# The first stage of an attention and two-layer feed-forward kernel, done by pairs of batches

## The chip, the cores and the metric

The kernel runs on one core of a Trainium2 chip. The metric is the device time of one execution in microseconds (us); several runs give a median. Five engines work side by side, each through its own instruction list in order: TensorE (PE in the rows; PEld is its weight load), VectorE (DVE), ScalarE (ACT), GpSimd (POOL) and SyncE (SP), which issues most transfers.

## The reference

Attention over 4 batches, 8 heads, 576 tokens and 64 channels, through 32 memory slots, feeds a gated feed-forward layer (1536 wide) and then a second layer (2048 wide). All in float32; the feed-forward weights arrive as 64-bit numbers.

```python
a = exp(phi - max(phi, axis=2)); a = a / (sum(a, axis=2) + 1e-09)
k_m = einsum('bhsm,bhsd->bhmd', a, k);  v_m = einsum('bhsm,bhsd->bhmd', a, v)
attn = softmax(q @ k_m.T / 8);          x = attn @ v_m          # to (2304, 512)
xn = x / sqrt(mean(x * x) + 1e-06) * rms_g
x = (silu(xn @ w_gate) * (xn @ w_val)) @ w_out
h = x @ w_in
g = where(h >= 1, h, where(h <= -1, 0, (h + 1) ** 2 / 4))
out = g @ w_out2
```

## The kernel before

**Precision.** A product of float32 matrices is made of three matmuls with operands split in a high and a low part: high by high, high by low, low by high. A 64-bit weight block of 512 KB (`raw`, four buffers) is turned into float32 by `convert` in four elementwise steps: high word scaled (line 271 or 273), low word scaled (276 or 278), merged (282), sign put in (287, always VectorE before, since `BIAS["VAsign"]` is 98.9). Where the weight is also split, ScalarE makes the high and VectorE the low part (301, 303).

**Attention.** For each batch b, `soft` takes the softmax numerators of phi, `memory` the products k_m and v_m, and `pair` handles 128 rows by two tokens of queries: scores, softmax, squares for the norm, and at last the normalized attention weights `Ah`, `Al` (transposes `ATp`, lines 717 to 728). There are eight full pairs and one for the last 64 tokens of all four batches (`RESTS`, `ORDER`).

**Gates.** The attention output is never formed. Instead v_m is multiplied into the gate and value weights: `vw` makes, from two weight chunks of 128 columns and one batch, the products `vwps` (line 772), which are split into `vwh` and `vwl`. `gv` multiplies these by `Ah`, `Al`: per batch and chunk two halves of 288 tokens, a `gps` and a `vps` group of 6 matmuls each (line 819). So there are 4 x 12 x 2 x 2 = 192 such groups, 1152 matmuls of 288 columns. `gate` applies the silu and at once splits the result into `ah`, `al` (lines 872 to 893), for which there are 12 buffers. The converted chunks are written to DRAM (`wf_d`) and read back for batches 1 to 3, 36 times 512 KB.

**out1.** Per batch, block of 128 output columns and half, a group of 36 matmuls of 288 columns (line 920), 1152 in all. `x2_parts` splits the result and writes it to DRAM. Meanwhile the second layer's weights are converted and written to `w_d` (`w2_piece`).

**Second stage.** `p2_in` (`hp`, line 1098) and `p2_out` (`acc`, line 1129) run over four blocks of 512 tokens and one of 256. Its weights come back through POOL's queue; twelve of them wait until the first stage's matrices have left their place (`w2b`).

**Order.** All of the first stage is written by one planner, `Agenda`: generator streams ask for an engine and a time, for buffers (`take`, `give`) or for flags, and the planner emits instructions in the order in which they could start by its own costs, ties by priority (`P_GV` 850, `P_OUT1` 900). The chip then runs each engine's list in that order. Before, weight loading begins after the exponentials of batch 3 (`W_AFTER`), and out1 after the attention.

Of the kernel before, what the change touches and what calls it, by code (L numbers as in the profile page):

```python
# [7 lines left out]
F32 = mybir.dt.float32  # L8
# [6 lines left out]
P = 128  # L15
# [8 lines left out]
BUFS = {"phi": 2, "kv": 2, "q": 2, "qr": 1, "pm": 1, "gm": 2, "s1": 2, "kd": 2, "qT": 2, "e": 4, "aT": 3, "half": 1, "raw": 4, "x": 2, "w": 3, "vw": 2, "a": 12, "th": 2, "xs": 3, "w2s": 2}  # L24
RESTS = [[0, 1, 2, 3]]
ORDER = [0, 1, 2, 3, 8, 4, 5, 6, 7]

BANKS = {"g": (0, 1), "v": (2, 3), "o": (4, 5), "p": (0, 1, 2, 3), "w": (6, 7), "q": (2, 3), "s": (1,), "x": (2, 3), "a": (0,), "t": (5,), "k": (7,), "m": (4,), "l": (4,)}

HEAT = (6, ('e', 2), 2.09, 0.34)  # L30
# [3 lines left out]
SHARE = {"VAhi", "VAsign", "Vs", "VGlo", "VGal", "GVe"}  # L34
# [8 lines left out]
Q_AT = [2, 6, 8, 9, 12]  # L43


class Agenda:
# [11 lines left out]
    def __init__(self, room):  # L58
        self.room = dict(room)
        self.turn = {}  # L60
        self.ticks = {}
        self.flags = {}
        self.free = {"D": 1.7}
        self.now = 0.0
        self.port = 0.0
        self.done = 0.0
        self.live = []
        self.count = 0
# [23 lines left out]
    def _start(self, x):  # L92
        kind, arg = x[3]
        at = x[4]
        if kind == "take":
            return (at, None) if self.room[arg] else None
        if kind == "flag":
# [18 lines left out]
    def run(self, stop=None):  # L116
        while self.live and not (stop and stop in self.flags):
# [14 lines left out]
            if kind == "take":  # L132
                self.room[arg] -= 1
            elif kind == "give":
                self.room[arg] += 1
            elif kind == "rest":
# [28 lines left out]
def tile_attn_moe(tc, q, k, v, phi, w_gate, w_val, w_out1, rms_g, w_in2, w_out2, out):  # L165
# [45 lines left out]
    def bank(tag, name):  # L211

        n = turn[tag] = turn.get(tag, -1) + 1
        z = BANKS[tag][n % len(BANKS[tag])]
        yield "take", ("bank", z)
        return psum.tile([P, 512], F32, tag=f"b{z}", name=name), ("bank", z)

    turn = {}
# [13 lines left out]
    keep = pool(right, "keep", "right")  # L232
# [5 lines left out]
    Ah = [keep.tile([P, 2, S], F32R, tag=f"Ah{b}", name=f"Ah{b}", bufs=1) for b in range(B)]  # L238
    Al = [keep.tile([P, 2, S], F32R, tag=f"Al{b}", name=f"Al{b}", bufs=1) for b in range(B)]

    agenda = Agenda({**BUFS, **{("bank", z): 1 for z in range(8)}})
# [9 lines left out]
    def convert(src, pieces, dst, split, done):  # L251
# [7 lines left out]
        nc.sync.dma_start(out=rs.rearrange("p (c f) -> p c f", c=pieces) if pieces > 1 else rs, in_=src)  # L259
        yield "rest", DMA_LAG  # L260
# [35 lines left out]
        if split:  # L296
            hi, lo = split
# [16 lines left out]

    apart = list(range(BUFS["w"], BUFS["w"] + BUFS["w2s"]))

# [31 lines left out]
    inputs = ExitStack()  # L348
    ld = pool(inputs, "ld", "left")
    st = pool(att, "st", "right")  # L350
    phi_t, kv_t, q_t = {}, {}, {}
    kmT_t = [st.tile([P, H, 2, M], F32, name=f"kmT{b}") for b in range(B)]
# [15 lines left out]
    def loads():  # L368

        seq = []  # L370
        for b in range(B):
            seq += [("phi", b), ("kv", b)]
        for i, pr in zip(Q_AT, q_loads, strict=True):
            seq.insert(i, ("q", pr))
        for s in seq:
            yield "take", "qr" if s[0] == "q" and s[1][0] == B else s[0]
# [5 lines left out]
            elif s[0] == "kv":  # L382
                b = s[1]
                t = kv_t[b] = ld.tile([P, 2, 4, J, D], F32, tag="kv", name=f"kv{b}", bufs=BUFS["kv"])
# [5 lines left out]
            else:  # L390
                b = s[1][0]
                yield "Dq", 3.4 if b < B else 0.45 * len(per_batch(s[1]))
                if b == B:
                    t = q_t[s[1]] = ld.tile([P, H, LJ, D], F32, tag="qr", name=f"qr{s[1][1]}", bufs=BUFS["qr"])
                    for bb, rows in per_batch(s[1]):
# [814 lines left out]
```

## Time and profile before

| | |
|---|---|
| median of 3 runs | 844.69 us (842.64 to 846.34) |
| span of the profiled execution, first to last instruction | 842.8 us |
| busy: PE, PEld, DVE, ACT, POOL | 97%, 85%, 53%, 40%, 10% |
| mean granted TensorE clock | 0.989 |
| moved by transfers | 137.54 MB |

The profiled execution has no run time of its own in the records, only its span; the median of the runs is 1.9 us above it. Two neighbouring matmuls overlap in the records, so the pace of a series is read from its length and count, and not from the duration of one.

### The profile page before, as it was taken

To read this page: it belongs to the slowest core of one execution; us is meant where nothing else is said; L and a number is where in the kernel's file an instruction comes from. 1 tells how busy PE (TensorE), PEld (TensorE's weight loads), DVE (VectorE), ACT (ScalarE), POOL (GpSimd) and SP (SyncE) were. 2 spreads that over 40 slices of the span, in tenths; PEclk is the share of its full clock that TensorE was granted. 3 is DMA by queue.
4 is the path that set the end of the run, shared out by engine and by line. 5 is a ranking of instruction groups with operands and counts; after the bars stand their busy time and mean duration, and the time that the engine had idled before them with its cause. 6 is when DMAs were issued, how large, how long until landed. Compare 5 with 4: busy or idle time off the path is not lost.

```text
span 842.8 us, 14911 instructions
## 1 busy us (share of the span) xinstructions
PE 819.2 (97%) x6052; PEld 719.6 (85%) x6052; DVE 450.7 (53%) x788; ACT 336.7 (40%) x635; POOL 82.6 (10%) x133
## 2 busy tenths in 40 slices
PE   7999879999999999999999999999999999999997
PEld 5887767999999998999998888888888888888896
DVE  3678898985775577558214333433343334333443
ACT  1558866763663356436203222222222222222232
POOL 3365400100000000001305100000000000000000
PEclk9999899999999999999999999999999999999999
DMA  9974697885789767886979900100040003000100
GB/s 319 323 248 134 217 313 259 301 281 182 241 281 305 237 217 261 265 265 224 327 233 343 368 1 1 51 1 0 10 141 0 1 1 101 0 1 1 51 1 25
DMA packets 76804, 137.54 MB, mean 163 GB/s; under 512 B 9408, under 2 KB 46272, under 8 KB 76736
## 3 DMA queue, kind: packets, MB, share of 16 engines
q1 hardware_dynamic: 66080, 108.02, 38.9%
q0 software_dynamic: 10496, 28.32, 10.6%
q8 instruction: 47, 0.77, 0.4%
q10 hardware_dynamic: 160, 0.26, 0.1%
q14 instruction: 21, 0.17, 0.1%
HBM read 99.35 MB, written 37.22 MB: 162 GB/s over the span
## 4 chain that ended last, share of the span: by engine, by line
PE 90%; DMA 5%; ACT 2%; DVE 2%; issue 1%; SPq 0%; ACTq 0%; DVEq 0%
PE acc L1129 24%; PE hp L1098 24%; PE ops L920 18%; PE vps L819 8%; PE gps L819 7%; PE vwps L772 2%; PE xp L693 2%; DMA raw<-in_moe_w_val_dram 2%; PE sc L630 2%; DMA raw<-in_moe_w_gate_dram 1%; DMA kv<-in_v_dram 1%; PE kvps L504 1%; DMA raw<-in_moe_w_out_dram 1%; PE qps L612 1%; PE heat L484 1%
## 5 line engine op out<-in xcount | busy, mean ns | idle before, releaser
L1098 PE MATMUL hp<-xh,w 128*128 128x512 f32 (+1 forms) x640 | 193.2, 368 | 0.0
L1129 PE MATMUL acc<-w,gh 128*128 128x512 f32 x576 | 178.4, 391 | 0.0
L1098 PEld LDWEIGHTS hp<-xh,w 128*128 128x128 f32 x640 | 117.0, 188 | 21.5
L1104 DVE SCALAR_TENSOR_TENSOR y<-y 128x512 f32<-128x512 f32 (+1 forms) x80 | 51.1, 638 | 151.4 <-ACT y L1103 151.4
L1129 PEld LDWEIGHTS acc<-w,gh 128*128 128x128 f32 x576 | 107.0, 188 | 22.5
L1098 PE MATMUL hp<-xl,w 128*128 128x512 f32 (+1 forms) x320 | 118.3, 370 | 0.0
L920 PE MATMUL ops<-ah,wo1h 128*128 128x288 f32 x384 | 113.7, 296 | 0.0
L920 PE MATMUL ops<-ah,wo1l 128*128 128x288 f32 x384 | 113.1, 295 | 0.0
L920 PE MATMUL ops<-al,wo1h 128*128 128x288 f32 x384 | 113.1, 294 | 0.0
L1129 PE MATMUL acc<-w,gl 128*128 128x512 f32 x288 | 112.6, 392 | 0.0
L1103 ACT ACTIVATE y<-hp,consts 128x512 f32<-128x512 f32 (+1 forms) x80 | 51.6, 645 | 151.2 <-PE hp L1098 151.2
L1113 ACT ACTIVATE gh<-y 128x512 fp32r<-128x512 f32 (+1 forms) x80 | 47.5, 593 | 137.4 <-PE acc L1129 120.0
L1114 DVE TENSOR_TENSOR gl<-y,gh 128x512 fp32r<-128x512 f32 (+1 forms) x80 | 51.1, 639 | 80.3 <-ACT gh L1113 80.3
L920 PEld LDWEIGHTS ops<-ah,wo1h 128*128 128x128 f32 x384 | 72.0, 188 | 2.5 <-issue 2.5
L920 PEld LDWEIGHTS ops<-al,wo1h 128*128 128x128 f32 x384 | 72.0, 188 | 0.0
L920 PEld LDWEIGHTS ops<-ah,wo1l 128*128 128x128 f32 x384 | 72.0, 188 | 0.0
L1098 PEld LDWEIGHTS hp<-xl,w 128*128 128x128 f32 x320 | 60.3, 188 | 10.7
L1129 PEld LDWEIGHTS acc<-w,gl 128*128 128x128 f32 x288 | 54.0, 188 | 12.3
L819 PE MATMUL vps<-Ah,vwh 128*128 128x288 f32 x192 | 59.6, 310 | 3.0 <-DVE th L875 2.9
L819 PE MATMUL gps<-Ah,vwh 128*128 128x288 f32 x192 | 58.3, 303 | 1.5 <-ACT th L872 1.5
L819 PE MATMUL gps<-Ah,vwl 128*128 128x288 f32 x192 | 57.3, 298 | 0.0
L819 PE MATMUL gps<-Al,vwh 128*128 128x288 f32 x192 | 57.2, 298 | 0.0
(123 smaller groups left out, 1258.1 us busy)
## 6 DMA issues: line engine op xcount, KB each, us to landing
w<-wf_d SPq DMA_DIRECT2D x36, 512.0 KB, 4.9
w<-w_d POOLq DMA_DIRECT2D x36, 512.0 KB, 10.5
w_d<-w2s SPq DMA_DIRECT2D x32, 512.0 KB, 3.9
raw<-in_moe_w_out_dram SPq DMA_DIRECT2D x28, 512.0 KB, 5.0
raw<-in_moe_w_in_dram SPq DMA_DIRECT2D x16, 512.0 KB, 5.5
raw<-in_moe_w_gate_dram SPq DMA_DIRECT2D x12, 512.0 KB, 5.2
raw<-in_moe_w_val_dram SPq DMA_DIRECT2D x12, 512.0 KB, 6.3
wf_d<-w SPq DMA_DIRECT2D x12, 512.0 KB, 4.0
```

Source lines behind the costliest of these rows:

```text
L484: nc.tensor.matmul(out=t[:, 0:256], lhsT=zeros[:, 0:P], rhs=zeros, start=True, stop=True, skip_group_check=True,)
L630: nc.tensor.matmul(out=scv[rows, z, :], lhsT=qT[:, h, rows], rhs=kmT_t[bb][:, z].rearrange("p j m -> p (j m)"), start=True, stop=True, ski ...
L693: nc.tensor.matmul(out=xp[rows, 256 * g : 256 * g + 256], lhsT=aT[:, i, g, rows], rhs=vbd_t[bb][:, g].rearrange("p h d -> p (h d)"), start ...
L772: nc.tensor.matmul(out=vps[g][0][32 * c : 32 * c + 32, 2 * P * x : 2 * P * x + 2 * P], lhsT=vT[b][hs, c, :], rhs=t[hs, c].rearrange("p i f ...
L819: nc.tensor.matmul(out=p[:, 0:HB], lhsT=wt[:, g, i, :], rhs=at[b][:, g, c], start=(g == 0 and x == 0), stop=(g == 1 and x == 2),)
L920: nc.tensor.matmul(out=p[:, 0:HB], lhsT=wt[:, fc, d], rhs=at[:, c], start=(fc == 0 and x == 0), stop=(fc == NF1 - 1 and x == 2),)
L1098: nc.tensor.matmul(out=hp, lhsT=wt[:, kc, :], rhs=xt[:, kc, 0:n], start=(kc == 0 and x == 0), stop=(kc == KC - 1 and x == 2),)
L1103: nc.scalar.activation(out=y, in_=hp, func=AF.Relu, scale=0.5, bias=half)
L1104: nc.vector.scalar_tensor_tensor(out=y, in0=y, scalar=1.0, in1=y, op0=ALU.min, op1=ALU.mult)
L1113: nc.scalar.activation(out=gh, in_=y, func=AF.Copy)
L1114: nc.vector.tensor_tensor(out=gl, in0=y, in1=gh.bitcast(F32), op=ALU.subtract)
L1129: nc.tensor.matmul(out=acc, lhsT=gt[:, cs], rhs=wt, start=(fc == 0 and x == 0), stop=(fc == NF2 - 1 and x == 2),)
```

## The change

Only the first stage is changed.

- `vw` takes one chunk and both batches of a pair (0 and 1, then 2 and 3); `gv` runs chunk by chunk over the two batches. A converted chunk is read back 12 times, not 36. Two `w` buffers remain of three.
- The last tokens are done by two pairs instead of one: for batches 0 and 1 after their own pairs, for 2 and 3 at the end.
- Loads follow `LOADS`: four weight blocks are asked for before phi, k and v of batch 2. Weight conversion may begin after the first batch's keys (`W_AFTER`).
- The sign step may go to ScalarE and POOL (`BIAS["VAsign"]` 0.5); it does so for 24 of 68 blocks.
- `soft` takes the maximum of phi by halving (`fold`, four operations) instead of one strided reduction.
- A gate stays unsplit, in the places of the inputs k, v and phi (`th_free`), and is split when out1 needs it (`splits`, three buffers `ab`). k and v of batch 2 have a place of their own, which becomes `Ah`, `Al` of batches 2 and 3 (`late`).
- out1 runs per batch over 512 tokens, all four output blocks at once in four banks, and at last over the 256 remaining tokens: 576 matmuls of 512 columns and 144 of 256. The results are written in 40 transfers instead of 96.
- Any free bank of a list is picked instead of the next in turn.

```diff
-RESTS = [[0, 1, 2, 3]]
-ORDER = [0, 1, 2, 3, 8, 4, 5, 6, 7]
...
+RESTS = [[0, 1], [2, 3]]
+ORDER = [0, 1, 2, 3, 8, 4, 5, 6, 7, 9]
...
-W_AFTER = [("e", 3)]
+W_AFTER = [("km", 0)]
...
-BIAS = {"VAhi": -0.0664, "GAlow": -0.8, "VGlo": 0.3, "VGsum": -99, "GVe": 0.8, "VGal": 0.3, "VAsign": 98.9, "VGvbd": -0.169}
+BIAS = {"VAhi": -0.0664, "GAlow": -0.8, "VGlo": 0.3, "VGsum": -99, "VGmax": 0, "GVe": 0.8, "VGal": 0.3, "VAsign": 0.5, "VGvbd": -0.169}
...
+LOADS = [
+    ("phi", 0), ("kv", 0), ("q", 0), ("phi", 1), ("kv", 1), ("q", 2), ("q", 4), ("raw", 3), ("phi", 2), ("kv", 2),
+    ("phi", 3), ("kv", 3), ("q", 5), ("q", 7), ("q", 9)
+]
...
+            if s[0] == "q":
+                add(-1, load_q(s))
+                continue
+            if s[0] == "raw":
+                yield "flag", s
+                continue
...
+                place = {"tag": "late", "bufs": 1} if b == 2 else {"tag": "kv", "bufs": BUFS["kv"]}
+                t = kv_t[b] = (late if b == 2 else ld).tile([P, 2, 4, J, D], F32, name=f"kv{b}", **place)
...
+        for z in range(BUFS["kv"]):
+            yield "take", "kv"
+            t = ld.tile([P, 9, SM], F32, tag="kv", name=f"kvth{z}", bufs=BUFS["kv"])
+            if z == 0:
+                rest.append(t.rearrange("p n s -> p (n s)")[:, 0 : NF1 * NL].rearrange("p (n s) -> p n s", n=NF1))
+            for y in range(6 if z == 0 else 0, 9):
...
+    def fold(name, x, to, op, kind):
+
+        eng = yield kind, (1.75, 3.2)
+        e = nc.vector if eng == "V" else nc.gpsimd
+        t = st.tile([P, 4, 4, M], F32, tag="half", name=f"half{name}", bufs=BUFS["half"])
+        e.tensor_tensor(out=t, in0=x[:, :, 0:4], in1=x[:, :, 4:8], op=op)
+        e.tensor_tensor(out=t[:, :, 0:2], in0=t[:, :, 0:2], in1=t[:, :, 2:4], op=op)
+        e.tensor_tensor(out=to, in0=t[:, :, 0], in1=t[:, :, 1], op=op)
+        e.tensor_tensor(out=to, in0=to, in1=x[:, :, 8], op=op)
+        yield "give", "half"
...
                     )
-        yield "give", "kv"
+        if b != 2:
+            yield "give", "kv"
+        else:
+            t = late.tile([P, 2, 2, 2, S], F32R, tag="late", name="late2", bufs=1)
+            for y, x in enumerate((Ah, Al)):
+                x.update({2: t[:, y, 0], 3: t[:, y, 1]})
+            mark("late")
...
     def vw():
 
-        for n in range(0, NT, 2):
-            b = n // NF1
-            yield "flag", ("vT", b)
+        for n in range(NP * NF1):
+            pb = n // NF1 * 2
             for x in range(2):
-                yield "flag", ("w", n + x)
...
+            yield "Pw", 1.05
+            t = w_t.pop(n)
             for x in range(2):
...
-
+        for n in range(NP * NF1):
+            fc = n % NF1
+            for x in range(2):
+                b = n // NF1 * 2 + x
+                if fc == 0:
+                    for jj in range(2):
+                        yield "flag", ("A", (b, jj))
...
+                for hf in range(2):
+                    if hf:
+                        yield "flag", ("A", (B, [b in r for r in RESTS].index(True)))
+                        yield "flag", ("th", 0)
...
+                    add(P_GV, gate(b, fc, hf, ps))
+                mark(("gv", b, fc))
+            yield "give", "vw"
...
+        for b in range(B + 1):
+            n = SM if b < B else NL
+            for fc in range(NF1):
+                for hf in range(2):
+                    yield "flag", ("g", min(b, B - 1), fc, hf)
+                yield "take", "ab"
+                t = p1x.tile([P, 2, SM], F32R, tag="ab", name=f"ab{b}_{fc}", bufs=BUFS["ab"])
+                ah, al = t[:, 0, 0:n], t[:, 1, 0:n]
+                src = th_t[b, fc] if b < B else rest[0][:, fc]
+                yield "A", 0.16 + n / 1150
+                nc.scalar.activation(out=ah, in_=src, func=AF.Copy)
+                add(P_GV, low_part(b, fc, src, ah, al))
...
     def out1():
-        for b in range(B):
-            for d4 in range(KC):
-                yield "flag", ("wo1", d4 // 2)
-                for hf in range(2):
-                    c = slice(HB * hf, HB * hf + HB)
-                    p, p_bank = yield from bank("p" if b == B - 1 and d4 else "o", f"ops{b}_{d4}_{hf}")
-                    for fc in range(NF1):
...
-                        d = slice(P * d4, P * d4 + P)
-                        for x, (wt, at) in enumerate(((wo1h, ah), (wo1h, al), (wo1l, ah))):
-                            nc.tensor.matmul(
-                                out=p[:, 0:HB], lhsT=wt[:, fc, d], rhs=at[:, c],
-                                start=(fc == 0 and x == 0), stop=(fc == NF1 - 1 and x == 2),
-                            )
-                        if d4 == KC - 1 and hf:
-                            add(P_OUT1, give("a"))
-                    add(P_OUT1, x2_parts(b, d4, hf, p[:, 0:HB], p_bank))
-
...
+            acc = []
+            for fc in range(NF1):
+                yield "flag", ("wo1", fc)
+                yield "flag", ("a", b, fc)
+                ah, al = a_t.pop((b, fc))
+                for d4 in range(KC):
+                    if fc == 0:
+                        acc.append((yield from bank("o", f"ops{b}_{d4}")))
+                    p, p_bank = acc[d4]
...
+                    if fc == NF1 - 1:
+                        add(P_OUT1, x2_parts(b, d4, n, p[:, 0:n], p_bank))
+                yield "give", "ab"
+
...
     add(P_VW, load_w())
-    for z in range(2):
-        for u in range(NF1 // 2):
```

The first place is SP's list, from the loads of the second batch's k and v on (`phi_381` before and `phi_604` of the change are phi of batch 2, `kv_402` and `kv_606` its k and v). Before:

```order
L381 DMA phi_381<-in_phi_dram 128x4x288
L402 DMA q_400<-in_q_dram 128x8x256
L387 DMA kv_402<-in_k_dram 128x4x576
L387 DMA kv_402<-in_v_dram 128x4x576
L396 DMA qr_585<-in_q_dram 32x8x128 x4
L402 DMA q_611<-in_q_dram 128x8x256
L381 DMA phi_711<-in_phi_dram 128x4x288
L387 DMA kv_713<-in_k_dram 128x4x576
L387 DMA kv_713<-in_v_dram 128x4x576
L402 DMA q_824<-in_q_dram 128x8x256
```

Of the change, where the first weight block, a query block and the last tokens' queries stand just ahead of these rows:

```order
L276 DMA raw_520<-in_moe_w_val_dram 128x4x256
L276 DMA raw_548<-in_moe_w_gate_dram 128x4x256
L276 DMA raw_574<-in_moe_w_val_dram 128x4x256
L276 DMA raw_589<-in_moe_w_gate_dram 128x4x256
L406 DMA phi_604<-in_phi_dram 128x4x288
L413 DMA kv_606<-in_k_dram 128x4x576
L413 DMA kv_606<-in_v_dram 128x4x576
L406 DMA phi_718<-in_phi_dram 128x4x288
L413 DMA kv_720<-in_k_dram 128x4x576
L413 DMA kv_720<-in_v_dram 128x4x576
L365 DMA wf_d<-w_388 128x1024
L447 DMA q_915<-in_q_dram 128x8x256
```

Four weight blocks, and a fifth that reuses the first one's buffer, now stand ahead of batch 2's phi, k and v, and the store of chunk 0 ahead of the last two query blocks.

The second place is TensorE's list in the gates, where the end of one group, one `vw` and the next work stand. Before (chunks `w_1564` and `w_1645`, batch 0's `vT_89`):

```order
L819 MATMUL vps_0_1756<-Al_97,vwh_1624 128x288
L819 MATMUL vps_0_1756<-Ah_93,vwl_1625 128x288
L772 MATMUL vwps_0_1763<-w_1564,vT_89 32x256 x4
L772 MATMUL vwps_1_1764<-w_1564,vT_89 32x256 x4
L772 MATMUL vwps_0_1763<-w_1645,vT_89 32x256 x4
L772 MATMUL vwps_1_1764<-w_1645,vT_89 32x256 x4
L819 MATMUL gps_1_1776<-Ah_93,vwh_1624 128x288
L819 MATMUL gps_1_1776<-Al_97,vwh_1624 128x288
L819 MATMUL gps_1_1776<-Ah_93,vwl_1625 128x288
```

Of the change (chunk `w_936`, `vT_92` and `vT_93` of batches 0 and 1):

```order
L875 MATMUL vps_2_1_1779<-Al_99,vwh_1553 128x288
L875 MATMUL vps_2_1_1779<-Ah_97,vwl_1554 128x288
L826 MATMUL vwps_0_1789<-w_936,vT_92 32x256 x4
L826 MATMUL vwps_1_1790<-w_936,vT_92 32x256 x4
L826 MATMUL vwps_0_1789<-w_936,vT_93 32x256 x4
L826 MATMUL vwps_1_1790<-w_936,vT_93 32x256 x4
L967 MATMUL ops_0_1819<-ab_0_1642,wo1h 128x512 x2
L967 MATMUL ops_0_1819<-ab_0_1642,wo1l 128x512
L875 MATMUL gps_3_0_1826<-Ah_96,vwh_1678 128x288
L875 MATMUL gps_3_0_1826<-Al_98,vwh_1678 128x288
```

The same four rows now use one chunk for two batches, and groups of out1 with 512 columns stand between the gates from the fourth chunk on.

## Rows read from the trace of the kernel before

**Rows 1.** The page's head and part 1: busy time, share, instructions.

```profile
span 842.8 us, 14911 instructions
PE 819.2 (97%) x6052; PEld 719.6 (85%) x6052; DVE 450.7 (53%) x788; ACT 336.7 (40%) x635; POOL 82.6 (10%) x133
```

**Rows 2.** Busy time by stretches: stretch, length, busy by engine, clock, DMA share, rate.

```profile
core 0: us, PE busy (x) PEld busy (x) DVE busy (x) ACT busy (x) POOL busy (x), PEclk, DMA share, GB/s
0.00:41.80 41.80, 35.28 (x520) 29.11 (x528) 20.47 (x42) 13.93 (x24) 14.53 (x35) 0.96 1.03 320
41.80:106.00 64.20, 59.03 (x778) 50.27 (x773) 50.38 (x99) 48.92 (x106) 34.79 (x45) 0.92 0.62 201
106.00:140.30 34.30, 28.27 (x269) 24.03 (x269) 30.90 (x58) 22.11 (x44) 0.00 (x0) 0.95 0.82 273
140.30:176.20 35.90, 35.90 (x388) 32.40 (x386) 32.25 (x58) 25.90 (x53) 3.05 (x4) 1.00 0.88 310
176.20:441.10 264.90, 264.25 (x2294) 254.73 (x2287) 157.98 (x284) 121.35 (x241) 13.68 (x22) 1.00 0.78 255
441.10:842.80 401.70, 396.45 (x1825) 329.02 (x1823) 158.71 (x250) 104.46 (x170) 16.55 (x28) 1.00 0.18 58
```

**Rows 3.** The chain that ended last, pieces: start, length, engine, tile, line, count.

```profile
213.40 0.80 PE gps L819 x6
215.00 0.79 PE gps L819 x6
243.31 1.02 PE vwps L772 x32
244.34 0.99 PE vps L819 x6
400.96 40.16 PE ops L920 x303
441.12 10.22 PE hp L1098 x45
460.21 2.72 PE acc L1129 x12
457.47 2.75 PE hp L1098 x12
800.89 1.44 PE hp L1098 x12
```

**Rows 4.** The chain between 92 and 140 us, its four longest pieces.

```profile
97.96 6.44 DMA raw<-in_moe_w_gate_dram
...
105.86 5.02 DMA raw<-in_moe_w_gate_dram
...
122.45 5.82 DMA raw<-in_moe_w_val_dram
...
129.07 6.92 DMA raw<-in_moe_w_val_dram
```

**Rows 5.** TensorE by line until 105.2 us, and the attention's last transposes.

```profile
L819 PE MATMUL gps<-Ah,vwh 128*128 128x288 f32 x10 | 3.9, 390 | 0.0
L819 PE MATMUL vps<-Ah,vwh 128*128 128x288 f32 x8 | 2.8, 349 | 0.0
L772 PE MATMUL vwps<-w,vT 64*32 64x256 f32 x64 | 2.2, 382 | 0.0
...
L717 PE MATMUL ATp<-ident,e x36: 272/273/329, 43.8 to 105.1; 128*128 128x128 f32 x36
```

**Rows 6.** TensorE and VectorE by line, 106 to 140.3 us.

```profile
L819 PE MATMUL vps<-Ah,vwh 128*128 128x288 f32 x27 | 9.1, 337 | 2.3 <-DVE th L875 2.2
L819 PE MATMUL gps<-Ah,vwh 128*128 128x288 f32 x26 | 8.4, 322 | 1.5 <-ACT th L872 1.5
L772 PE MATMUL vwps<-w,vT 64*32 64x256 f32 x112 | 4.2, 385 | 2.3 <-DVE w L287 2.3
L287 DVE SCALAR_TENSOR_TENSOR w<-raw,w 128x512 uint32<-128x512 uint32 x13 | 8.8, 682 | 0.0
```

**Rows 7.** VectorE, SP and POOL in order of time: start, length, line, operation.

```profile
34.22 0.68 DVE L646 TENSOR_TENSOR e<-sc,mx 128x512 f32<-128x512 f32 x1
41.78 0.69 DVE L640 TENSOR_REDUCE mx<-sc 128x16 f32<-128x512 f32 x1 [1.55 <-PE sc L630]
76.04 2.24 DVE L282 SCALAR_TENSOR_TENSOR w<-w,raw 128x512 uint32<-128x512 uint32 x2
76.23 1.50 POOL L664 TENSOR_TENSOR e<-e,sm 128x512 f32<-128x512 f32 x1
444.17 0.53 POOL L1031 DMA_DIRECT2D w<-w_d  x1 [26.86 <-PE hp L1098]
```

More of the change, by code (lines that the diff above doesn't have):

```diff
@@ L211, in bank @@
     def bank(tag, name):
-        n = turn[tag] = turn.get(tag, -1) + 1
-        z = BANKS[tag][n % len(BANKS[tag])]
-        yield "take", ("bank", z)
+        early = BANKS.get(tag + "0") if "attention" not in agenda.flags else None
+        z = yield "pick", early or BANKS[tag]
         return psum.tile([P, 512], F32, tag=f"b{z}", name=name), ("bank", z)
-    turn = {}
     base = pool(top, "base", "left")
@@ L296, in convert @@
         if split:
+            if place:
+                yield "take", place
+                split = split()
             hi, lo = split
@@ L406, in loads @@
-            add(0, arrived(s))
-        for name in ("phi", "kv", "q", "qr"):
-            for _ in range(BUFS[name]):
-                yield "take", name
-        mark("inputs")
+            add(0, arrived(s))
+        for z in range(BUFS["kv"]):
[4 more added lines that the diff above has]
+            for y in range(6 if z == 0 else 0, 9):
+                th_free.append(t[:, y])
+                yield "give", "th"
+            mark(("th", z))
@@ L582, in memory, with spread_v @@
         mark(("vT", b))
+    def spread_v(b, vs):
+        vbd = vbd_t[b]
+        for g in range(2):
+            eng = yield "VGvbd", (0.41, 0.62)
+            (nc.vector if eng == "V" else nc.gpsimd).tensor_tensor(
+                out=vbd[:, g],
+                in0=vs[:, g].unsqueeze(1).to_broadcast([P, 4, D]),
+                in1=mask.unsqueeze(2).to_broadcast([P, 4, D]),
+                op=ALU.mult,
+            )
+        mark(("vbd", b))
+        yield "give", "kd"
     def per_batch(pr):
@@ L966, in tile_attn_moe, with wo1_unit @@
-    wo1_left = [NF1 // 2, NF1 // 2]
+        rows, c = slice(P * d4, P * d4 + P), slice(SM * b, SM * b + n)
+        for x, dst in ((xh, x2h_d), (xl, x2l_d)):
+            yield "D", 0.7
+            nc.sync.dma_start(out=dst[rows, c], in_=x.bitcast(F32))
+        yield "rest", DMA_LAG
+        xs_free.append(tag)
+        yield "give", "xs"
+    def wo1_unit(fc):
+        if fc:
+            yield "flag", ("wo1 begun", fc - 1)
+        mark(("wo1 begun", fc))
+        src = wbits["out1"][P * fc : P * fc + P, :]
+        yield from convert(src, 1, None, (wo1h[:, fc], wo1l[:, fc]), lambda: mark(("wo1", fc)))
@@ L1005, in tile_attn_moe @@
         add(10**6, heat())
-    agenda.run("inputs")
-    inputs.close()
-    p1 = pool(left, "p1", "left")
-    th_free += [p1.tile([P, S], F32, name=f"th_{z}") for z in range(BUFS["th"])]
     add(P_GV, gv())
-    add(P_SOFT, more_places())
-    add(P_W2 - 1, more_w2s())
+    for b in range(2):
+        add(P_SOFT, more_xs(b))
     agenda.run("attention")
@@ L1076, in tile_attn_moe @@
     load_x(0)
-    for i in range(N2U, N2U + N2R):
-        load_w2(2 * i + 1, w2c)
     agenda.run()
```

360 lines of the change are left out of this document (161 added, 199 removed), and 5 rows, old and new, of the table BANKS.

## The prediction

> **What bounds the kernel now.** The page comes first: TensorE is busy 97% of the span [rows 1], but matmuls overlap in the records, so this doesn't show where it waits. The table of stretches splits the span where the work changes [rows 2]. From 441.1 us on runs the second stage, 401.7 us long, and the change doesn't touch it. From 140.3 us on TensorE is full in every stretch. What can be won lies in the attention, up to 106 us, in the stretch from 106 to 140.3 us, where it is busy 28.3 of 34.3 us, and in the pace of its full stretches.
>
> The pace is read from the chain [rows 3]. A gate group of 6 matmuls takes 0.797 us (0.80 and 0.79 in turn). A `vw` takes 1.02 us and makes the group behind it 0.19 us longer, so 1.21 us. In out1, 303 matmuls of 288 columns take 40.16 us, 132.5 ns each. In the second stage 12 matmuls of 512 columns take about 2.73 us, 227.5 ns each, and 12 of 256 columns 1.44 us, 120 ns.
>
> The last attention transposes start at 105.1 us; by then 54 gate matmuls (three times 10 and three times 8), 9 groups, and two `vw` (64 records of 32 each) have run [rows 5]. What was left: 183 groups x 0.797 = 145.9, 22 `vw` x 1.21 = 26.6, out1 1152 x 0.1325 = 152.7, together 325.2 us. It took from 105.2 to 441.1 us, 335.9 us. So TensorE waits 10.7 us behind the attention. Between 106 and 140.3 us stand 157 gate matmuls (the two lines shown with 27 and 26, four more with 26) and 112 records of `vw` [rows 6]: 26.2 x 0.797 + 3.5 x 1.21 = 25.1 us of work in 34.3, so 9.2 us of the 10.7 are lost there. Why: the chain runs through four weight loads of 5.0 to 6.9 us [rows 4], and 13 weight blocks are finished in the 34.3 us, one in 2.64 us [rows 6]. A chunk is two blocks and gives, for one batch, 4 groups and half a `vw`, 3.8 us; a block 1.9 us. 1.9 of 2.64 is 72%, and 25.1 of 34.3 is 73%: the gates run at the pace of the converted blocks.
>
> **The change part by part.**
>
> *One chunk for two batches.* A block now feeds 3.8 us of TensorE, so at 2.64 us a block the gates no longer starve. When the attention ends, both of VectorE's lists have finished about 12 blocks. Before, four of these six chunks were used up; now three are, and the other three hold about 23 us of gates. The wait behind the attention is bounded below by what the old kernel loses outside the starved stretch, 10.7 - 9.2 = 1.5 us, and above, without a new shortage, by the 10.7 us themselves. VectorE, ScalarE and TensorE are all asked for at once in the first pair's gates, as from 140.3 to 176.2 us, where VectorE is busy 32.3 of 35.9 us and TensorE never waits [rows 2]. I take 4 us, nearer to that row.
>
> *out1 in blocks of 512.* 1152 x 132.5 ns = 152.7 us becomes 576 x 227.5 + 144 x 120 ns = 131.0 + 17.3 = 148.3 us, 4.4 us less, all on the path, since TensorE is full there. The Trainium skill, in "TensorE: Matmul & The Clock Gate", section "Back-to-back issue gap", gives N/2.4 + 2.5 ns from one matmul of N columns to the next at 2.4 GHz; that is 122.5, 215.8 and 109.2 ns, and out1 would win only 1.1 us. By that rule the time would be 3.3 us above my sum; the rows, 10 to 12 ns a matmul slower, decide.
>
> *Work left after the attention.* The change has done 10 groups and three `vw` by its last transposes, by the order of its list. Left: 182 x 0.797 = 145.1, 21 x 1.21 = 25.4, out1 148.3, together 318.8 us, 6.4 less than 325.2 (4.4 of it out1).
>
> *The attention, with a tenth pair and early weights.* Its end is the open term. VectorE's list has the third pair's row maximum, at 41.8 us before [rows 7], behind about as much work in both kernels: the third batch's maximum is put behind it, and seven steps of conversion ahead of it. From there to its last operation of the attention come 118 operations instead of 100. The additional ones are mostly small (halves of the maximum, 64-token tails), so I count half the mean of 50.4 us / 99 for each, 4.5 us. Before, VectorE needed 64.2 us for 50.4 [rows 2], 78%. At that rate 54.9 us take 70, and the attention ends at 112 us; at the 90% of the next stretch (30.9 of 34.3) 61, and it ends at 103 us. I take 107, between them, 1.8 us later than before: conversions now fill early idle time, but the loads work the other way.
>
> *Order of loads.* SP's fifth weight block needs the first one's buffer, so SP waits for the last step of that conversion, which stands on VectorE six operations behind the second pair's exponent (34.2 us before [rows 7]), at about 37 us. Queued behind it on SP are phi, k and v of batches 2 and 3, 5.9 MB, at the 320 GB/s of the first stretch [rows 2] 18 us, so they are there at about 55 us. Attention work of batches 0 and 1 and of their last tokens covers this. Without that cover the delay falls on the attention's end, at most the 10 us between my 107 and 117.
>
> *Costed at nothing.* 24 fewer read-backs (12 MB) and fewer stores: behind 140.3 us the DMA share is 0.78 to 0.88 and TensorE is full [rows 2], so there was nothing to free. Splits taken apart from the gates, and a third ScalarE and VectorE piece per gate: VectorE is 158 of 265 us busy there [rows 2]. The last 84 us hold out1 alone (batches 2 and 3 and the last tokens), and each split has 12 matmuls, 2.73 us, to hide in; without that cover it costs its own ScalarE and VectorE step. The second stage starts on weights already there, 45 `hp` matmuls in 10.22 us without a gap [rows 3], and POOL's later loads wait for out1's end as before (444.2 us [rows 7]); four instead of three now stand behind the others. These are needed only in the ninth step, some 50 us later.
>
> **The sum.** 107 + 318.8 + 4 = 429.8 us instead of 441.1: 11.3 us less. The profiled span becomes 831.5 us, and with the 1.9 us by which the median of the runs stands above the span, 833 us.
>
> **The rivals.**
>
> *The attention is stretched.* For it: the wait on SP, a tenth pair, and VectorE at 78%. Against: batches 0 and 1 give work meanwhile. If it ends at 117 us, the second stage starts at 440 us and the time is 843 us, no change.
>
> *Slower: the first pair's gates starve.* In-order lists put gates behind conversion steps, and now out1's weights are converted in the same stretch. Left there are 86 groups and 9 `vw`, 79.5 us. At the old 73% they take 109 us, 29 more; with my 4 us taken out, the start is at 455 us and the time 858 us. It decides from a share of about 80% downwards: then 20 us of wait eat the 11.3 + 4 us and 4.2 more. Against it: stock and block pace, above.
>
> *VectorE is locked out by POOL.* Two merges (line 282) took 2.24 us at 76.04 us while POOL multiplied from 76.23 us for 1.50 us [rows 7]. Alone, at 0.68 each [rows 6], they take at most 1.4, so POOL cost about 1 us. The change gives POOL 24 more such multiplications. If each stops VectorE for 1 us and saves it 0.6 us, and all fall on the path, that is 24 x 0.4 = 10 us and 843 us. The Trainium skill's page "SBUF — State Buffer", section "SBUF: two separate sides", says the port pair shared by these two is an exclusive lock against VectorE operations with two SBUF inputs; by that rule, the row agrees. Against it as a whole: 18 of the 24 stand behind the attention, where VectorE has room.
>
> *The attention ends early*, at 95 us, because conversions already start among the first pairs: 821 us.
>
> **How the numbers follow.** Forecast 0.60 (its own range 825 to 840 us, by 103 to 112 us and 1.5 to 10.7 us, not both at their ends), stretched 0.18, starved 0.12, locked out 0.06, early 0.04. A difference of 0.5%, 4.2 us, is about what a measurement of this kernel tells from none: 840.5 and 848.9 us are the limits. Faster 0.67 (the forecast, the early end, and a stretched attention that ends below 114 us), same 0.20, slower 0.13. The range, 821 to 846 us, takes in the stretched and locked-out cases and leaves out the starved one and what is earlier than 821.
>
> **What would show it.** Right: the first `hp` near 430 us; out1's pace 227 ns; TensorE above 95% in the 80 us behind the last `ATp`, no weight load of 5 us and more in its chain there; that last `ATp` between 103 and 112 us. Wrong: an `ATp` behind 115 us, or VectorE as releaser of `gps` and `vps` groups for more than 15 us in all.

## The result and the profile after

The changed kernel takes 854.04 us (median of 4 runs, 851.98 to 854.94), the kernel before 845.52 us on the same chip. The ratio is 1.0111, 95% interval 1.0082 to 1.0139: 1.1% slower, where 833 us had been forecast. The profiled execution spans 852.8 us.

The page's head and part 1, for [rows 1]:

```profile
span 852.8 us, 14257 instructions
...
PE 827.6 (97%) x5644; PEld 691.8 (81%) x5644; DVE 443.6 (52%) x828; ACT 360.0 (42%) x720; POOL 123.0 (14%) x161
```

TensorE is again busy 97% of the span, and again this tells nothing about where the time went. The attention's last transposes, for [rows 5] (first and last start stand behind the durations):

```profile
L770 PE MATMUL ATp<-ident,e x40: 222/273/473, 43.0 to 118.0; 128*128 128x128 f32 x32, 64*128 64x64 f32 x8
```

The table of stretches, cut there, columns as in [rows 2]:

```profile
0.00:41.80 41.80, 35.20 (x522) 30.44 (x522) 20.86 (x51) 14.76 (x27) 16.66 (x36) 0.96 0.94 294
41.80:118.00 76.20, 66.88 (x816) 50.66 (x815) 52.92 (x113) 51.58 (x113) 45.69 (x52) 0.93 0.62 209
118.00:198.00 80.00, 80.00 (x699) 69.94 (x699) 69.73 (x141) 56.96 (x127) 12.04 (x9) 1.00 0.57 186
198.00:445.60 247.60, 243.52 (x1796) 211.71 (x1795) 141.01 (x275) 132.34 (x284) 29.94 (x32) 0.99 0.65 225
445.60:852.80 407.20, 401.99 (x1826) 329.09 (x1824) 159.08 (x252) 104.36 (x171) 18.71 (x32) 1.00 0.20 64
```

Three things are to be seen. The attention ends at 118.0 us, 12.9 us later than before. In the 80 us behind it TensorE doesn't pause at all, where it had been busy 28.3 of 34.3 us. And the second stage, whose code is the same, takes 407.2 us instead of 401.7.

From the attention's end to the first `hp` are 327.7 us instead of 335.9. The second stages, counted from their first `hp` at 441.0 and 445.7 us, differ by 5.3 us, and 12.9 - 8.2 + 5.3 makes the 10.0 us between the spans. The chain that ended last, in pieces as in [rows 3]:

```profile
63.26 6.69 DMA raw<-in_moe_w_val_dram
...
70.03 0.66 POOL raw L296
70.69 0.58 PE kvps L567 x4
...
396.68 30.25 PE ops L967 x132
...
472.25 2.80 PE acc L1163 x12
...
479.48 2.80 PE hp L1132 x12
...
568.73 2.76 PE hp L1132 x12
```

In the second stage 12 matmuls of `acc` and of `hp` take 2.80 us each in the first block, where 2.72 and 2.75 stood, and 2.80 and 2.76 in the later ones, where they took 2.76 and 2.73. In the attention the chain runs through a weight block: POOL's list has a conversion step (L296) ahead of attention work, the block comes late, and the matmuls that close the fourth batch's memory (L567) wait for POOL. How SP came to be late, its issues in order of time:

```profile
24.94 1.49 SPq L276 DMA_DIRECT2D raw<-in_moe_w_val_dram  x1
35.43 0.37 SPq L276 DMA_DIRECT2D raw<-in_moe_w_gate_dram  x1
35.91 0.45 SPq L406 DMA_DIRECT2D phi<-in_phi_dram  x1
36.40 0.51 SPq L413 DMA_DIRECT2D kv<-in_k_dram  x1
36.95 0.51 SPq L413 DMA_DIRECT2D kv<-in_v_dram  x1
```

The fifth block waits 8.9 us for VectorE's sign step, and phi, k, v of the third batch are issued behind it. The matmuls of the third memory start at 53.2 us (before: 41.7).

### The profile page after: what moved, and what is told of

It reads as the page before. It is cut to its first block, busy times and chain, and to the rows that moved or that the text cites. A ratio compares the mean times of both kernels' runs of the same rounds, so it can differ in the third digit from the quotient of the medians.

```text
span 852.8 us, 14257 instructions
## 1 busy us (share of the span) xinstructions
PE 827.6 (97%) x5644; PEld 691.8 (81%) x5644; DVE 443.6 (52%) x828; ACT 360.0 (42%) x720; POOL 123.0 (14%) x161
## 3 DMA queue, kind: packets, MB, share of 16 engines
q0 software_dynamic: 10496, 28.32, 10.7%
## 4 chain that ended last, share of the span: by engine, by line
PE 91%; DMA 2%; DVE 2%; ACT 1%; POOL 1%; issue 1%; SPq 0%; ACTq 0%; DVEq 0%; POOLq 0%
PE acc L1163 24%; PE hp L1132 24%; PE ops L967 17%; PE gps L875 9%; PE vps L875 8%; PE vwps L826 3%; PE sc L683 2%; PE xp L746 2%; DMA w_d<-w2s 2%; PE heat L528 1%; PE qps L665 1%; DMA raw<-in_moe_w_val_dram 1%; PE kvps L548 1%; PE ATp L770 1%; DVE phi L506 0%
## 5 line engine op out<-in xcount | busy, mean ns | idle before, releaser
L967 PE MATMUL ops<-ab,wo1h 128*128 128x512 f32 (+1 forms) x480 | 139.5, 376 | 0.4 <-DVE xs L983 0.4
L967 PEld LDWEIGHTS ops<-ab,wo1h 128*128 128x128 f32 x480 | 84.0, 190 | 18.1 <-issue 5.8
L967 PE MATMUL ops<-ab,wo1l 128*128 128x512 f32 (+1 forms) x240 | 89.1, 371 | 0.0
L967 PEld LDWEIGHTS ops<-ab,wo1l 128*128 128x128 f32 x240 | 45.5, 190 | 8.3 <-DVE wo1l L324 0.2
L1139 DVE TENSOR_TENSOR y<-y,hp 128x512 f32<-128x512 f32 (+1 forms) x80 | 50.6, 633 | 2.6
L312 POOL TENSOR_TENSOR cx<-cx,raw 128x512 f32<-128x512 f32 x18 | 26.2, 1458 | 152.9 <-ACT raw L310 115.9
L943 DVE TENSOR_TENSOR ab<-kvth,ab 128x512 fp32r<-128x512 f32 (+1 forms) x40 | 26.2, 657 | 40.2 <-ACT ab L938 40.2
L846 DVE TENSOR_TENSOR vwl<-vwps,vwh 128x512 fp32r<-128x512 f32 x48 | 33.0, 687 | 24.3 <-ACT vwh L844 24.2
L875 PE MATMUL gps<-late,vwh 128*128 128x288 f32 x192 | 40.1, 297 | 3.4 <-ACT kvth L904 3.4
L938 ACT ACTIVATE ab<-kvth 128x512 fp32r<-128x512 f32 (+1 forms) x40 | 22.7, 568 | 45.0 <-PE ops L967 44.8
```

What stands on the lines that cost most here:

```text
L312: nc.gpsimd.tensor_tensor(out=dst, in0=dst, in1=hv, op=ALU.mult)
L846: nc.vector.tensor_tensor(out=lv, in0=vps[g][0], in1=hv.bitcast(F32), op=ALU.subtract)
L875: nc.tensor.matmul(out=p[:, 0:HB], lhsT=wt[:, g, i, :], rhs=at[b][:, g, c], start=(g == 0 and y == 0), stop=(g == 1 and y == 2),)
L943: (nc.vector if eng == "V" else nc.gpsimd).tensor_tensor(out=al, in0=src, in1=ah.bitcast(F32), op=ALU.subtract)
L967: nc.tensor.matmul(out=p[:, 0:n], lhsT=wt[:, fc, d], rhs=at, start=(fc == 0 and x == 0), stop=(fc == NF1 - 1 and x == 2),)
L1139: nc.vector.tensor_tensor(out=y, in0=y, in1=hp, op=ALU.max)
```

## The experiments

Times without a label are from the profiled executions. "End" is the start of the last `ATp`, "start" that of the first `hp`.

**Does it belong to the program?** Both kernels once more.

> The changed kernel once more, to see which of its losses belong to the program. In its first profile the last transpose of the attention (ATp) starts at 118.0 us, where the kernel before has 104.7 to 105.1, and the 512-column matmuls of the second stage follow each other at 231 to 234 ns, where the kernel before has 227 to 230. Theory A (both belong to the program): ATp again within 1 us of 118.0, second stage again 407 us long, ratio 1.008 to 1.014. Theory B (the pace of the second stage is a matter of the execution): the second stage takes 402 to 407 us, and the steps are other ones than 231 to 234 ns.

> The kernel before once more, as the other half of the same question. Theory A: last ATp at 105 us, second stage 401.7 us, steps 226.6 to 230.2 ns. Theory B: the second stage is longer than 403 us here, and the steps move towards 233 ns.

Changed kernel: ratio 1.0096 (1.0068 to 1.0124), end 118.8, start 443.6, second stage 407.2 us. Kernel before: 103.8, 439.3, 401.9. Theory A holds, for the second stage to 0.2 us. The rest varies more. With the runs below that only move tiles of the second stage, five traces of the changed first stage have their end at 118.0 to 120.2 us and their start at 443.6 to 445.9, and three of the kernel before have 103.1 to 105.1 and 437.8 to 441.0. So a difference of 2 us at the end or the start of one trace tells nothing.

**The loads free, or POOL without multiplies.**

```diff
-    ..., ("q", 4), ("raw", 3), ("phi", 2), ("kv", 2),
+    ..., ("q", 4), ("phi", 2), ("kv", 2),
```

> The changed kernel without the one wait that holds the loads of the third and fourth batch behind the weight blocks, so that phi and k, v of the third batch are asked for ahead of the first weight block. Theory 1 (the fifth weight block, which waits on SP's list from 24.94 to 35.43 us for a buffer, makes the third batch's memory 11.5 us late, and this is the lateness of the attention): the matmuls of the third memory start near 42 us instead of 53.2, the last ATp at 106 to 110 us instead of 118.0, and the time falls by 8 to 11 us against the changed kernel. Theory 2 (the attention is late for its own work: a tenth pair, the sign multiplies on POOL and the waits for late weights): the memory comes early, but the last ATp stays at 114 us or later, and the time falls by less than 4 us.

```diff
-BIAS = {..., "VAsign": 0.5, ...}
+BIAS = {..., "VAsign": 98.9, ...}
```

> The changed kernel with all sign steps on VectorE, as in the kernel before: no multiply on POOL (24 of 1.3 to 1.5 us) and no Sign on ScalarE. The order of the loads on SP stays with the fifth weight block ahead of the third batch. Theory 1 (the lateness comes from SP's list): the last ATp moves by less than 3 us from 118.0. Theory 2 (POOL's multiplies stand before the attention's own POOL steps and before the weights' stores): the last ATp comes 4 to 8 us earlier, and the time falls by 4 to 8 us.

With free loads the third memory starts at 43.9 us, as expected, but the end comes at 116.9 us, the start at 445.6, and the ratio is 1.0118 (1.0095 to 1.0142): no gain. Theory 1 falls. But this kernel has a stop of TensorE of 4.34 us in the fourth memory (last section) that the changed kernel hasn't; without it the end would come at 112.6 us at the earliest, an estimate from these two numbers, still behind the 106 to 110 that theory 1 expected. With the sign steps on VectorE the end is 119.7, the ratio 1.0103 (1.0080 to 1.0127): POOL's multiplies, a part of theory 2, are not the cause. The chain of the kernel with free loads shows what its end hangs on:

```profile
99.98 5.43 DMA raw<-in_moe_w_val_dram
...
105.44 0.68 ACT w L289
106.11 0.49 ACT vwh L844
106.60 0.49 ACT late L781
...
108.69 0.28 ACT aT L729
...
109.02 1.95 PE xp L746 x16
```

Now it is ScalarE: a conversion step waits for a block that SP issued at 99.98 us, and the last pair's `aT` stands behind it.

**The attention alone.** The conversion of the weight blocks waits for its end (`W_AFTER = ["attention"]`, in the changed kernel with free loads); four blocks are still loaded. One execution of each kernel.

> The changed kernel with its weight blocks held back until the attention has ended (the loads of the third and fourth batch need no weight block here), so that the attention runs alone: no conversion, no vw, no gate before the last ATp. Its whole time is of no interest, only where the attention ends. Theory 2a (the tenth pair, the fold, the shared banks make the attention itself longer): the last ATp comes 6 us or more after that of the kernel before treated alike. Theory 2b (the attention alone is as long as before, and is stretched by the weight work that is put among it): within 3 us of it, and at 100 us or earlier.

> The kernel before with its weight blocks held back until the attention has ended, as the other half. Both theories: the last ATp earlier than 104 to 105 us, at 90 to 100; its distance to that of the changed kernel treated alike tells the theories apart.

The same line of `ATp`, for the changed kernel and for the one before:

```profile
L770 PE MATMUL ATp<-ident,e x40: 221/273/366, 47.6 to 108.8; 128*128 128x128 f32 x32, 64*128 64x64 f32 x8
```

```profile
L717 PE MATMUL ATp<-ident,e x36: 272/273/421, 44.2 to 93.8; 128*128 128x128 f32 x36
```

Without conversion and gates the changed attention is 15.0 us longer: theory 2a. The weight work adds 8 us to it (116.9 with the same loads), and 10 to 11 to the attention before, so the weight work by itself doesn't set the two apart. But not all of the 15.0 us is work of the attention. Only the trace with ten pairs has two stops of TensorE in its memories, of 1.23 and 4.26 us, with nothing waited for. The longer one:

```profile
62.24 1.10 PE L548 MATMUL kvps<-kv,phi 64*32 64x128 f32 x30 [4.26 <-issue]
```

And its last pair runs almost alone: TensorE, busy 3.4 of the 6 us before, has a granted clock of 0.50 from 100 us on (1.2 GHz), where the kernel before had 0.97 and more in its last pair.

**The tenth pair.**

```diff
-RESTS = [[0, 1], [2, 3]]
-ORDER = [0, 1, 2, 3, 8, 4, 5, 6, 7, 9]
+RESTS = [[0, 1, 2, 3]]
+ORDER = [0, 1, 2, 3, 8, 4, 5, 6, 7]
```

> The changed kernel with the last 64 tokens of all four batches in one pair of 128 rows, as in the kernel before (nine pairs instead of ten), all else as changed, the fifth weight block ahead of the third batch's loads too. Theory 2c (the tenth pair is what the attention is longer by): the last ATp 6 us or more earlier than 118 to 119, the time 4 to 7 us less. Theory 2d (the fold, the shared banks and the waits for instructions and weights make it longer; the pair itself lies in gaps): within 3 us of 118.

> The attention of the changed kernel alone (weight blocks held back until it has ended) with one pair for the last tokens: nine pairs, as in the kernel before, whose attention alone ended at 93.8 us, and with ten pairs at 108.8. Theory 2c: the last ATp at 100 us or earlier. Theory 2d: 104 us or later, the rest of the 15 us lying in the memories of the four batches and in the order of the pairs.

With nine pairs the end is 114.3 us, between the two expectations, the start 438.3, the ratio 1.0034 (1.0017 to 1.0050). The attention alone ends at 101.4 instead of 108.8, again between them. So 7.4 of the 15.0 us go with the tenth pair, of which up to 5.5 can be the two stops. The other 7.6 us lie in the last pair and not in the memories: the last but one's transposes start at 88.4 us (before 90.2), the last one's at 101.0 (before 93.4), behind scores at 85.7 us (before, the last scores come at 76.9 to 78.8). TensorE is busy 0.7 of the 4 us up to 92, and the clock granted from 92 to 98 us is 0.50 here too. No run took out the new maximum or the shared banks. What still holds the end of the whole kernel at 114.3, in its chain:

```profile
40.12 2.08 SPq L413
...
42.24 3.41 SPq L413
...
45.75 12.43 DMA wf_d<-w
58.17 0.00 POOLq L312
58.18 0.45 POOL s L469
...
58.67 0.39 PE kvps L567 x4
...
69.77 2.39 issue
```

SP issues the late k and v and behind them the store of a converted chunk, which takes 12.43 us. The profile puts a sign step in POOL's list (L312) down to that store; the softmax of phi (L469) and the close of the third memory (L567) come behind. A stop of 2.39 us follows.

**Both, and 96 bytes for the second stage** (below).

> The changed kernel with three things mended at once: the loads of the third and fourth batch do not wait for the weight blocks, one pair for the last tokens, 96 bytes ahead of the second stage's tiles. If each lateness that was named is the cause (theories 2c and C1), the last ATp comes at 105 to 110 us, the second stage takes 402 us, and the span is 832 to 838 us, ratio 0.987 to 0.996. If the attention is long for another reason, the last ATp stays at 114 or later and the ratio is 1.000 to 1.006.

The end is 103.7 us, among the 103.1 to 105.1 of the kernel before, with the new maximum and the shared banks still in. So the late loads and the tenth pair together are what the end was late by. Seen from 103.7, late loads alone give 114.3, the tenth pair alone 116.9, both 118.8: they overlap, and taking back one of them won only 1.9 and 4.5 us, both 15.1. A part of this is not theirs: the two kernels with one of the edits have stops of 4.34 and 2.39 us, which this one and the changed one lack. But the second stage starts only at 435.9 us and takes 405.9; the span is 841.7, above the 832 to 838 expected, and the ratio 1.0009 (0.9998 to 1.0020).

**The second stage: 32 bytes.** Its instructions are the same in both kernels, but three tiles lie elsewhere. A tile that nothing reads moves them; here 32 bytes:

```diff
+    gap = pool(right, "gap", "right").tile([P, 8], F32, name="gap")
+    nc.gpsimd.memset(gap, 0.0)
     xa = pool(right, "xa", "right")
```

> The changed kernel with a tile of 32 bytes per partition that nothing reads, set on the right side just before the second stage's tiles. The second stage's code is the same in both kernels, but the changed one puts gh, gl and the first block's x elsewhere: in the kernel before, each of its operands starts 32 bytes past a multiple of 64 in a partition, and in the changed one gh, gl and the first x start at a multiple of 64. The tile moves these three by 32 bytes and nothing else. Theory C (the places set the pace): the second stage takes 402 to 403 us instead of 407.2, its 512-column matmuls follow each other at 227 to 230 ns, the time falls by about 5 us. Theory D (the pace comes from something else in the program, such as the places of the weights or what the first stage leaves under way): it stays at 407 us and 231 to 233 ns.

> The kernel before with the same tile of 32 bytes, which here moves gh, gl and the first x to multiples of 64. Theory C: the second stage takes 406 to 408 us instead of 401.9, and the kernel is 4 to 6 us slower. Theory D: 402 us, no change.

The kernel before, with 32 bytes put in, from the table of stretches and from the chain:

```profile
437.80:845.00 407.20, 401.91 (x1825) 328.96 (x1824) 158.95 (x250) 104.77 (x170) 16.61 (x28) 1.00 0.18 57
```

```profile
563.61 2.80 PE acc L1131 x12
566.41 2.76 PE hp L1100 x12
```

That is the changed kernel's second stage, 407.2 us, with its 2.80 and 2.76 us, made in the kernel before by 32 bytes; ratio 1.0061 (1.0037 to 1.0085). Theory C holds here. In the changed kernel 32 bytes give 405.2 us, not the 402 to 403 expected, and 1.0092 (1.0067 to 1.0116), so the rule is finer.

> The changed kernel with 96 bytes instead of 32 ahead of the second stage's tiles. The 32 bytes took the kernel before from 401.9 to 407.2 us in its second stage, the changed one only from 407.2 to 405.2. With 96 bytes gh, gl and the first x start 96 bytes past a multiple of 128, as in the kernel before and as the weights of the second product do in both. Theory C1 (the start within 128 bytes, against that of the weights, decides): the second stage takes 401 to 403 us, the span is 5 us below the changed kernel's, the ratio to the kernel before 1.001 to 1.007. Theory C2 (32 of 64 bytes is what matters, and the rest of the 5.3 us has another cause): 405 us as with 32 bytes.

> The changed kernel with 480 bytes ahead of the second stage's tiles: gh, gl and the first x start 480 bytes past a multiple of 512, which is where they start in the kernel before (its 32-byte version, at 448 past a multiple of 512 like the changed kernel, had the changed kernel's steps to the nanosecond). Theory C3 (where they start within 512 bytes sets the steps): the second stage takes 401.9 us, 0 to 0.5 more, with steps of 226.6 to 230.2 ns, and the span is 5 us below the changed kernel's 850.8 to 852.8. Theory C4 (other places matter too, those of the weights among them): 404 to 407 us.

With 96 bytes it is 405.8 us, ratio 1.0095 (1.0080 to 1.0110): C1 falls. With 480 bytes:

```profile
445.90:847.90 402.00, 396.77 (x1826) 329.27 (x1824) 159.01 (x252) 104.28 (x171) 18.75 (x32) 1.00 0.20 65
```

402.0 us and 1.0046 (1.0027 to 1.0065): theory C3. The starts of gh, gl and the first x in bytes past a multiple of 512, with the second stage's time:

| start | second stage |
|---|---|
| 480 (kernel before; 480 bytes put in) | 401.9, 402.0 us |
| 448 (changed kernel; kernel before with 32) | 407.2 us |
| 416 (changed kernel with 32) | 405.2 us |
| 352 (changed kernel with 96) | 405.8 us |

Equal starts within 512 bytes give equal times in different kernels; equal starts within 128 (480 and 352) don't, and 256 was not told from 512. The attention's end here is 120.2 us, so this is the second stage's share of the loss alone.

**Put together, and what is left.**

> The mended kernel (loads of the third and fourth batch not behind the weight blocks, one pair for the last tokens) with 480 instead of 96 bytes. Its attention ended at 103.7 us, its second stage began at 435.9 and took 405.9. Theory C3: second stage 401.9 us, span 836 to 839 us, ratio to the kernel before 0.993 to 0.998, faster than both kernels. Theory C4: span 840 to 843, ratio 0.998 to 1.002.

> The same with all sign steps on VectorE, none on POOL. If POOL's multiplies cost (POOL holds back the attention's own steps or VectorE), the last ATp or the start of the second stage comes 2 us or more earlier than in the mended kernel. If they help (VectorE is the engine that feeds the gates), the start of the second stage comes 2 us or more later than 435.9.

> The same as the mended kernel with 480 bytes, but the first weight block waits for the fourth pair's exponentials, as in the kernel before, instead of the first memory. If the early weight blocks are worth something, the second stage starts 2 us or more later than in the mended kernel (435.9); if they only stand in the way of the attention, the last ATp comes earlier than 103.7 and the second stage starts no later.

With 480 bytes the mended kernel takes 841.55 us, ratio 0.9963 (0.9951 to 0.9976), span 838.9: faster than both kernels, as theory C3 expected, by less than the forecast for the change. Its stretches:

```profile
104.40:140.30 35.90, 34.72 (x322) 29.32 (x321) 33.30 (x64) 26.81 (x60) 7.60 (x6) 1.00 0.66 216
140.30:436.90 296.60, 292.76 (x2211) 253.87 (x2209) 188.93 (x365) 161.34 (x353) 33.97 (x35) 0.99 0.66 223
436.90:838.90 402.00, 396.75 (x1826) 329.26 (x1824) 159.14 (x252) 104.52 (x171) 18.75 (x32) 1.00 0.20 65
```

Sign steps on VectorE: end 110.4, start 438.2, ratio 0.9971 (0.9958 to 0.9984). So POOL's multiplies don't hold anything back; without them the end is 6 us later, and a block waits again (7.85 us in the chain at 102.29). Late weight blocks: end 106.0, start 438.1, ratio 0.9963 (0.9948 to 0.9977). By the letter of the expectations both starts, 2 us and a little more behind 435.9, say that the multiplies help and that the early blocks are worth something; but they are 1.3 and 1.2 us behind the 436.9 of the kernel compared with, less than the start varies, and the ratios are equal within their intervals. The runs tell no worth of either.

```diff
+    pool(left, "gapx", "left").tile([P, 80], F32, name="gapx")
     xb = pool(left, "xb", "left")
```

> The mended kernel with 480 bytes, and 320 bytes more ahead of the later blocks' x, which in all kernels so far start 160 bytes past a multiple of 512; with them they start at 480, as the first block's x and gh, gl do. In the first block, where x and gh start alike, the matmuls of the second product follow each other at 226.6 ns and those of the first at 228.9; in the later blocks at 230.2 and 227.7. Theory C5 (tiles that start alike give the first block's steps everywhere): the second stage takes 399.5 to 401 us instead of 402.0. Theory C6 (the later blocks' steps have another cause than the start of x): 402 us, or another number with no pattern of the first block.

The chain of its later blocks:

```profile
560.62 2.72 PE acc L1166 x12
563.34 2.75 PE hp L1135 x12
```

These are the first block's steps of [rows 3]. The second stage takes 400.1 us, the kernel 838.69 us, ratio 0.9935 (0.9916 to 0.9955). Theory C5 holds, and this is the fastest version.

## Why the prediction was wrong

The forecast span was 831.5 us, the measured one 852.8. The 21.3 us, step by step, each rounded:

| step | forecast | measured | difference |
|---|---|---|---|
| the attention's end | 107 | 118.0 | 11.0 |
| from there to the first `hp` | 318.8 + 4 | 327.7 | 4.9 |
| the second stage | 401.7 | 407.2 | 5.5 |

**The attention's end** is the step that failed: forecast between 103 and 112 us, it came at 118.0, behind the 115 us that the prediction itself had named as the sign of being wrong. VectorE's work was sized rightly: 54.9 us forecast, 52.9 us measured from 41.8 us on. The rate wasn't: VectorE is busy 69% of that stretch, less than before, so it was not what the attention waited for.

Two terms failed, and together they make 15.1 us: with both taken back the end is where the kernel before has it. The tenth pair, costed with the new maximum at 4.5 us of VectorE, costs 13.2 us when the loads are free (103.7 against 116.9, up to 4.3 of it the stop of TensorE in that kernel). "Attention work of batches 0 and 1 and of their last tokens covers this" put the late loads at nothing. They came when forecast (third memory at 53.2 us, forecast about 55), but the cover held only in part: freeing them won 1.9 us with ten pairs, no more than two traces of one kernel differ by, or up to 6.2 without that stop, and 10.6 with nine (103.7 against 114.3, up to 2.4 of it a stop), where the one pair of last tokens needs batches 2 and 3 and covers nothing. What share of the 11.0 us each term has, the runs don't tell. The chains show how steps hold each other up: conversion steps stand ahead of attention steps in ScalarE's and POOL's lists, and a step whose block is late stops both. This is the rival of the stretched attention, with the wait on SP and the tenth pair for it, and nearly its 117 us; its 843 us lacked the other two terms.

**The second stage** was costed at nothing, since the change "doesn't touch it". It moved three of its tiles. The two paces in [rows 3], 2.72 and 2.75 us for equal matmuls, were a sign that something sets them, but no row of before showed what.

**Work and wait behind the attention.** The pairing did what it was to do: TensorE is full for 80 us behind the attention (forecast: above 95%), and busy 78.42 of the 79.6 us behind it in the mended kernel with 480 bytes, so the starved rival is out. out1 needs 30.25 / 132 = 229.2 ns a matmul of 512 columns; with 120 ns for the short ones that is 576 x 0.2292 + 144 x 0.120 = 149.3 us, a gain of 3.4 us where 4.4 were forecast and an estimate by the formula of the Trainium skill's "TensorE: Matmul & The Clock Gate", section "Back-to-back issue gap", gave 1.1. That section gives the formula for an isolated matmul, and about 131 ns for 512 columns in a stream with weight loads; the 229.2 ns here agree with neither. So the work left was 319.8 us, and the wait 7.9 us in this execution and 5.0 in the second (324.8 in all), within the bounds of 1.5 to 10.7 us. This step was sized nearly rightly.

With the end repaired the wait is larger. In the mended kernel with 480 bytes, 184 groups, 22 `vw` and out1 are 146.6 + 26.6 + 149.3 = 322.5 us; it takes 332.5, 10.0 us of wait. So of the 14.4 us won at the attention's end against the second execution (118.8 to 104.4), 2.8 are work not yet done by then and 5.0 come back as wait; 6.7 remain at the start of the second stage. Half of the 10.0 us are idle TensorE in the two stretches (1.2 + 3.8); where the other half goes stays open. So with the attention's end at 104.4 us and the old second stage the span is 838.9 us, and not 831.5.

**VectorE locked out by POOL**, at a net 0.4 us a step: not borne out. Taking out all 24 multiplies moved the time by nothing measurable in the changed kernel, and the end the wrong way in the mended one. The Trainium skill's rule of the shared port ("SBUF — State Buffer", "SBUF: two separate sides") may still hold for single operations; these runs test only the sum.

## What to carry to other kernels

A step that waits for a transfer, put into an engine's in-order list ahead of other work, stops that work too: look at what stands behind each such step, on every engine and on the queue that issues the loads, and take an average busy share for no limit unless the engine is what is waited for. Two delays that overlap hide each other: taken back singly they won 1.9 and 4.5 us, together 15, so take suspects back together as well as one by one. When a stage's code is unchanged, compare its pace anyway, and look at where its tiles start.

## What was not expected of the hardware

**The start of a tile sets the pace of matmuls.** The same 1,824 matmuls of the second stage took 400.1, 401.9, 405.2, 405.8 or 407.2 us, by where a few of its tiles start within 512 bytes, at a granted clock of 1.00 each time; the three of these times that were profiled more than once repeat to 0.2 us. In the second product one matmul follows the other after 226 to 227 ns throughout in the fastest version and after 230 to 236 ns in the changed kernel, in a pattern that repeats with each piece of 12; equal starts of x, gh and gl gave the shortest time. The Trainium skill's page "SBUF — State Buffer", section "Operand start alignment", states which starts are allowed, and says that its runs timed nothing; these runs did. Why the starts matter isn't shown.

**TensorE stops in the middle of a list of equal matmuls.** In the kernel with free loads, 114 of the fourth memory's 144 small matmuls run, then nothing for 4.34 us, and the profile names no releaser:

```profile
55.37 1.86 PE kvps L548 x114
57.23 4.34 issue
61.57 1.10 PE kvps L548 x30
```

In the same kernel the transfers between 55 and 63 us, in 40 slices of 0.2 us, and the queue of the instructions:

```profile
DMA  8989999999999999999550100000000000000000
...
q8 instruction: 1, 0.02, 0.9%
```

The stop ends after the transfers of the weight blocks do, and one packet of the instruction queue comes in it. Such stops have a fixed place. The nineteen traces have 26 stops of TensorE over 0.6 us behind which the next instruction waits for no semaphore, all in the first 73 us. Counting the matmuls, weight loads and waits that a trace records for TensorE, each stop comes after 193 of them more than a multiple of 256: after 449 in every trace, after 1,729 here and in the attention alone with ten pairs (there a shorter one after 1,217 too), after 1,985 in the kernel with nine pairs and late loads. So it isn't these matmuls that stop but a place in the list, and an edit that moves instructions moves what stands there. The Trainium skill's page "Runtime: NRT & Kernel Launch", section "Instruction fetch mechanics", says that instructions are fetched in blocks of 16 KiB, 256 instructions, and that the cost of crossing into the next is mostly hidden. The count agrees with such blocks; up to 4.34 us were not hidden. That the block came late behind the full queue of transfers is argued, not shown.
